# Two reorderings in a split-precision transformer kernel: curve ahead of weight decoding in four steps, and weight sums in two parts

## The chip, the core and the metric

The kernel runs on one core of a Trainium2 chip. The core has a matrix engine (TensorE, PE in the profile, with its weight loads shown apart as PEld), VectorE (DVE), ScalarE (ACT), GpSimd (POOL) and a queue for transfers (SP). Each engine works through its own list of instructions in the order in which the program gives them; an instruction that waits holds up all that stand behind it on that engine. The metric is the device time of one execution in microseconds (us), and less is better.

## The reference, cut to what matters

Three parts follow each other. Shapes are fixed: 2 batches, 8 heads, 768 positions, head width 64, so 1536 tokens of width 512.

```python
def reference(q, k, v, moe_w_in, moe_w_out, moe2_w1, moe2_w2, moe2_w3, moe2_w_out):
    x = local_attention_with_block_summaries(q, k, v)     # [1536, 512]
    h = x @ moe_w_in                                      # [1536, 2048]
    x = (h - tanh(h)) @ moe_w_out                         # [1536, 512]
    a, b = x @ moe2_w1, x @ moe2_w2                       # [1536, 1024] each
    return ((a * b) @ moe2_w3) @ moe2_w_out               # [1536, 512]
```

All of it is in 32-bit floating point.

## The kernel before, in words

**Split products.** TensorE multiplies in a shorter format, so each factor is held as a high part (the value cast down, names ending in `h`) and a low part (what the cast lost, names ending in `l`). A product is three matrix multiplications of 128 x 128 by 128 x 512, high x high, high x low, low x high (`split_mm`, L185 to L188). ScalarE makes a high part, and GpSimd or VectorE subtracts it to make the low part (`low_part`, L190). Where a factor comes from TensorE, both parts must be there before its three multiplications can run: the high part for the first, the low part for the second or the third.

**Weights.** The weights arrive as 64-bit words and are decoded on the chip. The class `Weights` (object `wt`) holds one list of units in the order in which they are needed. One unit is a transfer into a `raw` buffer (a ring of four: a new transfer waits until the decoding of the unit four earlier is over), a first step on ScalarE (L108, in `start`), three on VectorE (L111, L113, L115, in `dve` and `unit`), a cast on ScalarE (L143, in `high`) and a subtraction on GpSimd (L150, in `low`). Nothing schedules this: a unit stands on each engine where the program calls these methods.

**First stage (attention, to about 128 us).** Groups of tiles go through scores, softmax and values, with weight units decoded between them: `wt.start` begins one in each turn of the loop and `wt.dve(1)` three times a turn puts one VectorE step of it between the softmax steps.

**Middle stage (about 128 us to 445 us).** 48 steps, one for each pair of a block of 128 hidden columns `f` and a third of the tokens `k`. Step `n` calls `hidden(n)`: 12 multiplications on TensorE into one of three banks, named `ph`. `curve(n, ...)` then computes h - tanh(h): ScalarE squares (`u`, L530) and takes tanh (`th`, L531), and makes `sq` (L538) and a mask `mk` (L539); VectorE forms a polynomial `g` for small values (L540 to L542) and overwrites it where the mask says so (COPY_PREDICATED, L525). That last operation is put off to the beginning of `curve(n + 1)`, and after it come the high part `gh` of g on ScalarE (L535) and the low part `gl` on GpSimd (L191). `back(n - 2)`, 12 multiplications named `x`, uses them; so TensorE's order is hidden(0), hidden(1), hidden(2), back(0), hidden(3), back(1), hidden(4), and so on. In the first four steps every `hidden` needs a new w_in unit and, from step 2 to step 5, every `back` a new w_out unit; the next new units are needed in step 12.

In the order of the code a step does: `hidden`, `wt.start`, `wt.high`, the reading of finished x banks (`evacuate`), `curve`, `wt.low`, `back`. Inside `curve`, a whole unit is decoded on VectorE (`wt.unit()`, L526) between the predicated copy and the rest.

**Last stage (from about 458 us).** For two of the three thirds of the tokens, a and b are computed with a seven-product scheme in place of eight. `group` (L715) makes one of them, for two blocks of columns: it calls seven products in the order 1, 6, 5, 7, 2, 4, 3, each 6 multiplications into one of four banks named `p_w`, in rotation. VectorE adds a bank to what is to become a block of the result, right behind each product. Product 3 takes the bank that product 5 had; it is read twice, the second time by `tt(c22, c21, add, p5)` (tiles `ab` in the trace), which comes behind product 7. `w_sums` (L689) makes the sums of weights that the next group multiplies with: two operations `t_w` of 512 columns on VectorE, then four of 256 columns (`s_w`), then a cast on ScalarE and a subtraction on GpSimd for each of two results. Products 6 and 5 use the first result, 7 and 3 the second. Group w1 and group w2 alternate for m = 0, 2, 4, 6; both need sums, and each group's sums are made while the group ahead of it runs, directly behind its `yield` after product 5: seven times in all (those of the very first group are made earlier). `between` puts 12 other multiplications (`o`) behind product 5 where there is something to do: in the first group, and from m = 2 in both.

## Time and profile before

| | us |
|---|---|
| median of three runs | 592.7 (590.75 to 592.89) |
| the profiled execution, its own time | 592.24 |
| its span, first to last instruction | 590.4 |
| TensorE busy in the span | 571.6 |
| VectorE busy | 465.4 |
| ScalarE busy | 338.6 |
| GpSimd busy | 278.9 |

The span is the stretch that the trace shows; the execution's own time is 1.84 us longer. A busy share is a mean over stages of different kinds. TensorE's multiplications overlap, and the end that is shown of each is modelled: a multiplication of 512 columns is shown as 0.39 us long, while in a row of them one begins every 0.23 us. In the timeline the bracket behind a row is the engine's idle time ahead of it and what ended that.

### The profile page before, as it was taken

To read this page: it belongs to the slowest core of one execution; us is meant where nothing else is said; L and a number is where in the kernel's file an instruction comes from. 1 tells how busy PE (TensorE), PEld (TensorE's weight loads), DVE (VectorE), ACT (ScalarE), POOL (GpSimd) and SP (SyncE) were. 2 spreads that over 40 slices of the span, in tenths; PEclk is the share of its full clock that TensorE was granted. 3 is DMA by queue.
4 is the path that set the end of the run, shared out by engine and by line. 5 is a ranking of instruction groups with operands and counts; after the bars stand their busy time and mean duration, and the time that the engine had idled before them with its cause. 6 is when DMAs were issued, how large, how long until landed. Compare 5 with 4: busy or idle time off the path is not lost.

```text
span 590.4 us, 9062 instructions
## 1 busy us (share of the span) xinstructions
PE 571.6 (97%) x3168; PEld 461.4 (78%) x3168; DVE 465.4 (79%) x885; ACT 338.6 (57%) x741; POOL 278.9 (47%) x233
## 2 busy tenths in 40 slices
PE   8989999998999999999999999999999999999997
PEld 6667777776888888888888888888887777888885
DVE  3789988789999995779999978999577576878510
ACT  3689977868788774466767667765233322222110
POOL 3456555555556652224645522557735624526120
PEclk9989999998999999999999999999999999999999
DMA  8899996653333230012223102223000100000021
GB/s 323 297 323 306 333 298 226 188 162 111 104 108 108 73 106 1 0 37 73 95 84 101 43 1 64 80 71 108 1 0 1 72 0 1 1 2 0 1 90 53
DMA packets 19678, 59.70 MB, mean 101 GB/s; under 512 B 2096, under 2 KB 4784, under 8 KB 19632
## 3 DMA queue, kind: packets, MB, share of 16 engines
q1 hardware_dynamic: 19632, 59.12, 30.8%
q8 instruction: 25, 0.41, 0.3%
q14 instruction: 21, 0.17, 0.1%
HBM read 54.79 MB, written 3.15 MB: 98 GB/s over the span
## 4 chain that ended last, share of the span: by engine, by line
PE 76%; DVE 14%; issue 6%; POOL 2%; ACT 1%; DMA 1%; DVEq 0%; POOLq 0%; ACTq 0%
PE x L187 6%; PE x L188 6%; PE x L186 6%; PE ph L187 6%; PE ph L188 6%; PE ph L186 6%; PE p_w L186 3%; PE p_w L187 3%; PE p_w L188 3%; PE o L188 3%; PE o L186 3%; PE o L187 3%; PE s L339 2%; PE busy L403 2%; PE w L188 2%
## 5 line engine op out<-in xcount | busy, mean ns | idle before, releaser
L150 POOL TENSOR_TENSOR wl<-dec,wh 128x512 fp32r<-128x512 f32 x72 | 111.5, 1553 | 48.9 <-ACT wh L143 41.6
L191 POOL TENSOR_TENSOR gl<-g,gh 128x512 fp32r<-128x512 f32 x48 | 65.8, 1371 | 140.5 <-ACT gh L535 75.3
L186 PE MATMUL x<-gh,wh 128*128 128x512 f32 x192 | 75.4, 393 | 1.8 <-ACT gh L535 1.8
L187 PE MATMUL x<-gl,wh 128*128 128x512 f32 x192 | 75.5, 393 | 1.0 <-POOL gl L191 1.0
L188 PE MATMUL x<-gh,wl 128*128 128x512 f32 x192 | 75.4, 393 | 0.0
L186 PE MATMUL ph<-xh,wh 128*128 128x512 f32 x192 | 74.8, 390 | 0.0
L187 PE MATMUL ph<-xl,wh 128*128 128x512 f32 x192 | 74.7, 389 | 0.0
L188 PE MATMUL ph<-xh,wl 128*128 128x512 f32 x192 | 74.7, 389 | 0.0
L115 DVE SCALAR_TENSOR_TENSOR dec<-raw,dec 128x512 uint32<-128x512 uint32 x45 | 62.4, 1387 | 1.5
L530 ACT ACTIVATE u<-ph 128x512 f32<-128x512 f32 x48 | 28.8, 600 | 54.8 <-PE ph L188 54.8
L143 ACT CAST wh<-dec 128x512 fp32r<-128x512 f32 x72 | 44.5, 623 | 13.3 <-DVE dec L115 13.2
L540 DVE TENSOR_TENSOR g<-ph,u 128x512 f32<-128x512 f32 x48 | 32.7, 682 | 19.8 <-ACT th L531 19.8
L525 DVE COPY_PREDICATED g<-mk,th 128x512 f32<-128x512 uint32 x48 | 41.7, 870 | 4.0
L186 PEld LDWEIGHTS x<-gh,wh 128*128 128x128 f32 x192 | 36.5, 190 | 10.3 <-ACT gh L535 2.2
L353 ACT ACTIVATE pr<-pr,nm 128x120 f32<-128x120 f32 x96 | 37.0, 390 | 12.1 <-DVE nm L350 11.8
L187 PEld LDWEIGHTS x<-gl,wh 128*128 128x128 f32 x192 | 36.4, 189 | 9.0 <-POOL gl L191 1.3
L188 PEld LDWEIGHTS x<-gh,wl 128*128 128x128 f32 x192 | 36.4, 190 | 7.5
L187 PEld LDWEIGHTS ph<-xl,wh 128*128 128x128 f32 x192 | 36.1, 188 | 7.5
L186 PEld LDWEIGHTS ph<-xh,wh 128*128 128x128 f32 x192 | 36.0, 188 | 7.5
L188 PEld LDWEIGHTS ph<-xh,wl 128*128 128x128 f32 x192 | 36.1, 188 | 7.4
L542 DVE SCALAR_TENSOR_TENSOR g<-sq,g 128x512 f32<-128x512 f32 x48 | 40.3, 839 | 0.7 <-ACT sq L538 0.6
L191 POOL TENSOR_TENSOR s_w<-s_w,s_w 128x512 fp32r<-128x512 f32 x16 | 20.4, 1292 | 38.9 <-ACT s_w L704 36.0
(153 smaller groups left out, 1423.0 us busy)
## 6 DMA issues: line engine op xcount, KB each, us to landing
raw<-w SPq DMA_DIRECT2D x32, 512.0 KB
raw<-w_in SPq DMA_DIRECT2D x16, 512.0 KB
raw<-w_out SPq DMA_DIRECT2D x16, 512.0 KB
vg<-vW SPq DMA_DIRECT2D x8, 768.0 KB
raw<-wo SPq DMA_DIRECT2D x8, 512.0 KB
kt<-kT SPq DMA_DIRECT2D x7, 544.0 KB
vn<-vN SPq DMA_DIRECT2D x8, 384.0 KB
qt<-qT SPq DMA_DIRECT2D x7, 384.0 KB
```

Of the source, the lines that this page charges most:

```text
L115: lambda tu=tu, su=su, lo=lo: stt(out=tu, in0=lo, scalar=29, in1=su, op0=ALU.logical_shift_right, op1=ALU.bitwise_or)])
L143: nc.scalar.copy(out=h, in_=self.t[n])
L150: nc.gpsimd.tensor_tensor(out=l, in0=self.t[self.n_low], in1=h[:, :].bitcast(F32), op=ALU.subtract)
L186: mm(out=acc, lhsT=lh, rhs=rh, start=start, stop=False)
L187: mm(out=acc, lhsT=lh, rhs=rl, start=False, stop=False)
L188: mm(out=acc, lhsT=ll, rhs=rh, start=False, stop=stop)
L191: eng.tensor_tensor(out=out, in0=x, in1=high.bitcast(F32), op=ALU.subtract)
L353: nc.scalar.activation(out=pr[g][:, i, :], in_=pr[g][:, i, :], func=AF.Exp, scale=-1.0, bias=nm[g][:, i:i + 1], accum_out=z[g][:, i:i + 1])
L525: nc.vector.copy_predicated(out=g, mask=mask[:, :].bitcast(U32), data=t)
L530: nc.scalar.activation(out=u, in_=ph, func=AF.Square)
L540: nc.vector.tensor_tensor(out=gn, in0=ph, in1=u, op=ALU.mult)
L542: nc.vector.scalar_tensor_tensor(out=gn, in0=sq, scalar=GAM, in1=gn, op0=ALU.add, op1=ALU.mult)
```

## The change

The change touches three places.

In the attention's last turn no weight unit is begun and no VectorE step of one is put between the softmax steps.

In the first four steps of the middle stage (`FIRST = 4`), `curve` stands ahead of `wt.start`; the high and low parts of the step before follow directly behind the predicated copy, ahead of the new `u` and `th`; and no unit is decoded inside `curve`. Steps 2 and 3 decode one unit each behind `curve`, and steps 0 and 1 none; `wt.high` is called from step 2 on. From step 4 on all is as it was.

In the last stage `w_sums` is a generator in two parts. The two `t_w` operations stand where they were; the four `s_w`, with the casts and subtractions behind them, follow only after product 7 has been added and the bank of product 5 has been read.

```diff
+FIRST = 4
...
-                    if i:
+                    if i and g < NG + 3:
                         wt.dve(1)
...
-                wt.start(2 if g in MORE else 1)
+                if g < NG + 3:
+                    wt.start(2 if g in MORE else 1)
...
         def curve(n, ph, prev):
 
+            def high():
+                gp[n - 1] = tmp("gh", n, LAG + 1, F32R), tmp("gl", n, LAG + 1, F32R)
+                nc.scalar.copy(out=gp[n - 1][0], in_=g)
+                low_part(nc.gpsimd, gp[n - 1][1], g, gp[n - 1][0][:, :])
+
             if prev is not None:
                 mask, t, g = prev
                 nc.vector.copy_predicated(out=g, mask=mask[:, :].bitcast(U32), data=t)
-            wt.unit()
+                if n < FIRST:
+                    high()
+            if n >= FIRST:
+                wt.unit()
...
-            if prev is not None:
-                gp[n - 1] = tmp("gh", n, LAG + 1, F32R), tmp("gl", n, LAG + 1, F32R)
-                nc.scalar.copy(out=gp[n - 1][0], in_=g)
-                low_part(nc.gpsimd, gp[n - 1][1], g, gp[n - 1][0][:, :])
+            if prev is not None and n >= FIRST:
+                high()
...
+            if n < FIRST:
+                cur = curve(n, nxt, cur)
             wt.start()
...
-            wt.high()
+            if LAG <= n < FIRST:
+                wt.unit()
+            if n >= LAG:
+                wt.high()
             closing = len(evac)
             evacuate()
-            cur = curve(n, nxt, cur)
+            if n >= FIRST:
+                cur = curve(n, nxt, cur)
             wt.low()
...
             for t, h, l in ((t0, h0, l0), (t1, h1, l1)):
                 tt(t, h[:, :].bitcast(F32), add, l[:, :].bitcast(F32))
+            yield
             a, b = slice(0, H * P), slice(H * P, DM)
...
-            return lhs
+            yield lhs
...
             next(g)
-            lhs = w_sums("w2", m)
-            for _ in range(4):
+            sums = w_sums("w2", m)
+            next(sums)
+            next(g)
+            lhs = next(sums)
+            for _ in range(3):
                 next(g, None)
...
-            if m + 2 < NM:
-                lhs = w_sums("w1", m + 2)
+            more = m + 2 < NM
+            if more:
+                sums = w_sums("w1", m + 2)
+                next(sums)
             for a, b in ((a22, b22), (a11, b11), (a21, b21)):
                 next(g)
+                if more and a is a22:
+                    lhs = next(sums)
                 tt(a, a, ALU.mult, b)
```

The order on TensorE and on SP is the same before and after. On ScalarE, at the beginning of the middle stage, this stands before (numbers behind names only tell buffers apart; `dec_1943` and `dec_1958` are the w_out units of back(2) and back(3), `wh_1948` that of back(1)):

```order
L143 CAST wh_1948<-dec_1903 128x512
L108 ACTIVATE dec_1958<-raw_1896 128x512
L108 ACTIVATE dec_1997<-raw_1901 128x512
L143 CAST wh_1999<-dec_1943 128x512
L530 ACTIVATE u_2007<-ph_1984 128x512
L531 ACTIVATE th_2009<-ph_1984 128x512
L538 ACTIVATE sq_2008<-u_2007,nsb 128x512
L539 ACTIVATE mk_2010<-u_2007,numax 128x512
L108 ACTIVATE dec_2033<-raw_1941 128x512
L143 CAST wh_2035<-dec_1958 128x512
L530 ACTIVATE u_2044<-ph_2020 128x512
L531 ACTIVATE th_2046<-ph_2020 128x512
```

And this stands there after (`wh_2071` further down is now the cast of `dec_1943`):

```order
L144 CAST wh_1948<-dec_1903 128x512
L540 ACTIVATE u_1990<-ph_1977 128x512
L541 ACTIVATE th_1992<-ph_1977 128x512
L546 ACTIVATE sq_1991<-u_1990,nsb 128x512
L547 ACTIVATE mk_1993<-u_1990,numax 128x512
L109 ACTIVATE dec_2002<-raw_1896 128x512
L527 CAST gh_2018<-g_1994 128x512
L540 ACTIVATE u_2022<-ph_2004 128x512
L541 ACTIVATE th_2024<-ph_2004 128x512
```

The first `u` has moved ahead of two first steps of units and of a cast that waits for VectorE, and the first `gh` ahead of the second `u`.

On VectorE, at the same place before, behind the decoding of back(1)'s unit:

```order
L111 TENSOR_SCALAR dec_1943<-dec_1943 128x512
L191 TENSOR_TENSOR xl_122<-av_1920,xh_119 128x256
L113 SCALAR_TENSOR_TENSOR dec_1943<-raw_1853,dec_1943 128x512
L115 SCALAR_TENSOR_TENSOR dec_1943<-raw_1853,dec_1943 128x512
L111 TENSOR_SCALAR dec_1958<-dec_1958 128x512
L113 SCALAR_TENSOR_TENSOR dec_1958<-raw_1896,dec_1958 128x512
L115 SCALAR_TENSOR_TENSOR dec_1958<-raw_1896,dec_1958 128x512
L540 TENSOR_TENSOR g_2011<-ph_1984,u_2007 128x512
L541 TENSOR_TENSOR th_2009<-ph_1984,th_2009 128x512
L542 SCALAR_TENSOR_TENSOR g_2011<-sq_2008,g_2011 128x512
L525 COPY_PREDICATED g_2011<-mk_2010,th_2009 128x512
```

After, from the polynomial of step 1 to the predicated copy at the head of step 3 (that of step 0 stands ahead in the same way, with nothing of a unit in front of it):

```order
L548 TENSOR_TENSOR g_2026<-ph_2004,u_2022 128x512
L549 TENSOR_TENSOR th_2024<-ph_2004,th_2024 128x512
L550 SCALAR_TENSOR_TENSOR g_2026<-sq_2023,g_2026 128x512
L532 COPY_PREDICATED g_2026<-mk_2025,th_2024 128x512
L548 TENSOR_TENSOR g_2058<-ph_2036,u_2054 128x512
L549 TENSOR_TENSOR th_2056<-ph_2036,th_2056 128x512
L550 SCALAR_TENSOR_TENSOR g_2058<-sq_2055,g_2058 128x512
L112 TENSOR_SCALAR dec_1943<-dec_1943 128x512
L114 SCALAR_TENSOR_TENSOR dec_1943<-raw_1853,dec_1943 128x512
L116 SCALAR_TENSOR_TENSOR dec_1943<-raw_1853,dec_1943 128x512
L532 COPY_PREDICATED g_2058<-mk_2057,th_2056 128x512
```

The two units that stood ahead of the first polynomial now stand behind the third and the fourth; all later units follow three steps later than they did.

On VectorE in the last stage, group w2 of m = 0, this stands before (`p_w_0_5085` is the bank of product 5, `p_w_0_5110` that of product 7):

```order
L668 TENSOR_TENSOR b_5067<-b_5067,p_w_0_5085 128x512
L668 TENSOR_TENSOR t_w_2_5093<-wh_4214,wl_4215 128x512
L668 TENSOR_TENSOR t_w_2_5094<-wh_4332,wl_4333 128x512
L668 TENSOR_TENSOR s_w_2_5095<-t_w_2_5094 128x256
L668 TENSOR_TENSOR s_w_2_5095<-s_w_2_5095,t_w_2_5093 128x256
L668 TENSOR_TENSOR s_w_2_5096<-t_w_2_5093,t_w_2_5094 128x256
L668 TENSOR_TENSOR s_w_2_5096<-t_w_2_5093,s_w_2_5095 128x256
L668 TENSOR_TENSOR b_5067<-b_5067,p_w_0_5110 128x512
L668 TENSOR_TENSOR ab_1_4969<-b_5067,p_w_0_5085 128x512
L668 TENSOR_TENSOR ab_0_4968<-ab_0_4968,ab_1_4969 128x512
```

And after (product 7's bank is now `p_w_0_5099`):

```order
L682 TENSOR_TENSOR b_5067<-b_5067,p_w_0_5085 128x512
L682 TENSOR_TENSOR t_w_2_5093<-wh_4214,wl_4215 128x512
L682 TENSOR_TENSOR t_w_2_5094<-wh_4332,wl_4333 128x512
L682 TENSOR_TENSOR b_5067<-b_5067,p_w_0_5099 128x512
L682 TENSOR_TENSOR ab_1_4969<-b_5067,p_w_0_5085 128x512
L682 TENSOR_TENSOR s_w_2_5095<-t_w_2_5094 128x256
L682 TENSOR_TENSOR s_w_2_5095<-s_w_2_5095,t_w_2_5093 128x256
L682 TENSOR_TENSOR s_w_2_5096<-t_w_2_5093,t_w_2_5094 128x256
L682 TENSOR_TENSOR s_w_2_5096<-t_w_2_5093,s_w_2_5095 128x256
L682 TENSOR_TENSOR ab_0_4968<-ab_0_4968,ab_1_4969 128x512
```

The four `s_w` have moved behind the second reading of product 5's bank; the product of a and b (`ab_0_4968`), and the additions behind it, keep their places behind the sums. In the groups w1 the same two rows change places with the four, and in the first of them two copies of finished outputs move ahead with them.

## Rows read from the trace of the kernel before

**Rows 1.** The page's busy times of the engines, us, share of span, instructions.

```profile
PE 571.6 (97%) x3168; PEld 461.4 (78%) x3168; DVE 465.4 (79%) x885; ACT 338.6 (57%) x741; POOL 278.9 (47%) x233
```

**Rows 2.** Waits of TensorE: line, whom for, us in total, times, longest.

```profile
PE p_w L186 <- DVE ab L668: 3.2, 3, 1.4
PE x L186 <- ACT gh L535: 1.8, 1, 1.8
```

**Rows 3.** Stretches: length, busy us of each engine, granted clock, DMA share.

```profile
137.00:144.72 7.72, 4.94 (x15) 3.50 (x13) 7.38 (x12) 5.86 (x11) 3.47 (x3) 0.78 0.36 132
140.50:144.00 3.50, 3.50 (x9) 2.72 (x10) 3.36 (x7) 2.16 (x5) 1.65 (x1) 0.52 0.40 138
...
150.00:200.00 50.00, 50.00 (x222) 41.43 (x221) 48.42 (x65) 41.08 (x73) 29.51 (x20) 1.00 0.32 95
```

**Rows 4.** Timeline of TensorE, first steps of the middle stage: start, length, instruction.

```profile
131.40 0.39 PE L188 MATMUL ph<-xh,wl 128*128 128x512 f32 x1
...
136.84 0.39 PE L188 MATMUL ph<-xh,wl 128*128 128x512 f32 x1
...
144.72 0.39 PE L186 MATMUL ph<-xh,wh 128*128 128x512 f32 x1
```

**Rows 5.** Timeline of ScalarE, first steps of the middle stage.

```profile
133.45 0.59 ACT L530 ACTIVATE u<-ph 128x512 f32<-128x512 f32 x1
...
135.03 0.72 ACT L539 ACTIVATE mk<-u,numax 128x512 f32<-128x512 f32 x1
...
138.32 0.62 ACT L535 CAST gh<-g 128x512 fp32r<-128x512 f32 x1 [0.52 <-DVE g L525]
```

**Rows 6.** Timeline of VectorE, first steps, and the decoding of a later unit.

```profile
133.99 1.67 DVE L115 SCALAR_TENSOR_TENSOR dec<-raw,dec 128x512 uint32<-128x512 uint32 x1
...
136.78 0.68 DVE L542 SCALAR_TENSOR_TENSOR g<-sq,g 128x512 f32<-128x512 f32 x1
137.56 0.73 DVE L525 COPY_PREDICATED g<-mk,th 128x512 f32<-128x512 uint32 x1
...
165.13 0.41 DVE L111 TENSOR_SCALAR dec<-dec 128x512 uint32<-128x512 uint32 x1
...
166.30 0.69 DVE L115 SCALAR_TENSOR_TENSOR dec<-raw,dec 128x512 uint32<-128x512 uint32 x1
```

**Rows 7.** Timeline of GpSimd, first steps of the middle stage.

```profile
139.02 1.43 POOL L191 TENSOR_TENSOR gl<-g,gh 128x512 fp32r<-128x512 f32 x1 [3.91 <-DMA raw<-w_out]
```

**Rows 8.** Timeline of TensorE in the last stage, where product 3 begins.

```profile
469.35 0.39 PE L188 MATMUL p_w<-xh,wl 128*128 128x512 f32 x1
470.63 0.50 PE L186 MATMUL p_w<-xh,s_w 128*128 128x512 f32 x1 [0.90 <-DVE ab L668]
...
481.41 0.50 PE L186 MATMUL p_w<-xh,s_w 128*128 128x512 f32 x1 [0.87 <-DVE ab L668]
...
495.42 0.50 PE L186 MATMUL p_w<-xh,s_w 128*128 128x512 f32 x1 [1.38 <-DVE ab L668]
```

**Rows 9.** Timeline of VectorE in the last stage, two groups.

```profile
475.16 0.69 DVE L668 TENSOR_TENSOR b<-u_b,p_w 128x512 f32<-128x512 f32 x1 [2.15 <-PE p_w L188]
...
478.48 0.42 DVE L668 TENSOR_TENSOR s_w<-t_w 128x256 f32<-128x256 f32 x1
...
479.95 0.68 DVE L668 TENSOR_TENSOR b<-b,p_w 128x512 f32<-128x512 f32 x1
480.67 0.69 DVE L668 TENSOR_TENSOR ab<-b,p_w 128x512 f32<-128x512 f32 x1
481.39 1.83 DVE L668 TENSOR_TENSOR ab<-ab,ab 128x512 f32<-128x512 f32 x1
...
494.68 0.69 DVE L668 TENSOR_TENSOR ab<-a,p_w 128x512 f32<-128x512 f32 x1
```

**Rows 10.** Timeline of ScalarE, then GpSimd, in the last stage.

```profile
479.40 1.29 ACT L704 CAST s_w<-s_w 128x512 fp32r<-128x512 f32 x2 [5.13 <-DVE s_w L668]
...
480.15 2.52 POOL L191 TENSOR_TENSOR s_w<-s_w,s_w 128x512 fp32r<-128x512 f32 x2 [9.57 <-ACT s_w L704]
```

More of the change, by code (lines that the diff above doesn't have):

```diff
@@ L749, in fused_kernel @@
                 wt.free += [(rawp, "raw", "raw", NRAW)] * NRAW
-                lhs = w_sums("w1", 0)
+                _, lhs = w_sums("w1", 0)
             a = product_a(m, 0)
```

## The prediction

> **What bounds the kernel now.** I read the busy times first. TensorE is busy for 571.6 of 590.4 us [rows 1], so only its idle or slow time can be gained; the other engines matter where it waits for them. The waits of TensorE come second: of those that the change touches, three at product 3 (3.2 us, for the second reading of product 5's bank) and one at the first `back` (1.8 us, for `gh`) stand out [rows 2]. The stretches are third, since a wait can also cost clock: from 137.00 to 144.72 us TensorE is busy for 4.94 of 7.72 us at a mean granted clock of 0.78, and from 140.50 to 144.00 the clock is 0.52, its lower level (1.2 GHz); before and from 144 us on the trace shows 1.00 [rows 3]. Last come the timelines of the four engines around these two places [rows 4 to 10].
>
> **First steps of the middle stage.** From one last multiplication of a `hidden` to the next but one are 24 multiplications, 131.40 to 136.84, so one begins every 0.227 us, and 12 take 2.72 [rows 4]. hidden(2) leaves its last place at 136.84 + 0.23 = 137.07, and hidden(3) begins at 144.72. back(0) needs 2.72 of these 7.65 us; 4.93 are lost: 2.78 idle (7.72 less 4.94 [rows 3]) and some 2.1 at the lower clock.
>
> What TensorE waits for begins with `u` at 133.45 [rows 5], although hidden(0)'s last multiplication ended at 131.40 + 0.39 = 131.79 [rows 4]: `u` stood behind a cast that waited for a unit on VectorE, and VectorE's polynomial stood behind one more, whose last step took 1.67 us from 133.99 [rows 6]. Both units are needed only by back(2) and back(3). The change takes both out of the way. I follow the new chain with the durations of before.
>
> Step 0: `u` begins at 131.83. `mk` begins 1.58 later (135.03 less 133.45) and ends 0.72 after that, at 134.13 [rows 5]. VectorE's third operation needs `sq`, which I put at 0.62 ahead of `mk`'s end; so it starts at about 133.66, and the predicated copy 0.78 later (137.56 less 136.78), ending after 0.73, at 135.17 [rows 6]. `gh` follows 0.03 later and takes 0.62: 135.82. `gl` starts 0.70 behind the start of `gh` and takes 1.43 [rows 5, 7]: 137.33. back(0)'s first multiplication, due at 137.07, has its `gh`; the second, due at 137.30, has its `gl` at 137.37. About 0.1 us is lost in place of 4.93.
>
> Steps 1 to 3: from `u` to the next `u` is 3.9 (the 3.37 to `gh`, and ScalarE's next place 0.53 on), less than the 5.44 that TensorE gives to a step. So `u` starts at 135.7 and 139.6, and gl(1) ends at 141.2, for a place at 142.5. The third polynomial ends at 142.1; now the unit of back(2) comes on VectorE: from the first step to the end of the last 1.86 (166.30 + 0.69 less 165.13), or 2.84 where the last step takes 1.67 [rows 6]. I take 1.86, because GpSimd has nothing between gl(1) and this unit. Then come copy and `gh`, to 145.4, and on GpSimd the unit's low part first, 144.7 to 146.0, and gl(2) to 147.4, for a place at 148.2: 0.8 to spare, or 0.2 late. Step 3 in the same way: `u` 145.3, polynomial 147.8, unit 149.7, copy 150.4; but now ScalarE has the cast, a unit's first step, `u` and `th` of step 4 ahead of gh(3) (step 4 has the old order), to 152.4; and gl(3) to 153.9, for a place at 153.7. Here 0.2 is lost, 1.2 if both units took the longer time. Together 0.3 lost, bounds 0.1 and 3.8 (0.1 + 0.2 + 1.2 + a slow clock as before, 2.1, with 0.2 for its restart): this part gains **4.6**, between 1.1 and 4.8.
>
> Behind step 3 VectorE's work per step is as before, and nearly all its time (48.42 of 50.00 us [rows 3]); since it starts with TensorE, both are earlier by the same amount. The units come three steps later than they did. The order on GpSimd shows that each low part stands at least two steps, 10.9 us, ahead of its use. The transfers wait for a raw buffer and shift with the units: that for step 4 is released at 144.0, and ScalarE asks for it at about 150. Cost zero, hidden by these distances. Leaving out the unit at the attention's end moves three VectorE operations out of a stretch where TensorE isn't waiting: zero, with 0.2 either way.
>
> **Last stage.** In a row a multiplication is shown 0.39 long but takes 0.23, so each wait costs the idle time, 0.16, and 0.11 for the slower start (its 0.34 to the next in place of 0.23, from rows like that of 470.63). The three cost 0.90, 0.87 and 1.38 plus 0.27 each [rows 8]: 1.17, 1.14 and 1.65, together 3.96. What is moved is four operations, 478.48 to 479.95, 1.47 us [rows 9].
>
> In group w1 of m = 0 the second reading ends 1.47 earlier, at 469.1, and product 3 is due at 469.35 + 0.23 = 469.58 [rows 8]: nothing is left of the wait. In w2 of m = 0 it ends at 480.67 + 0.69 - 1.47 = 479.9, for a place at 480.4: nothing left. So TensorE reaches w1 of m = 2 earlier by 2.31. There the reading ended at 494.68 + 0.69 = 495.37 [rows 9]. VectorE runs nearly without a gap from w2 of m = 0 to this point, and its chain begins with a wait of 2.15 for TensorE [rows 9]; so it comes 1.17 earlier, and 1.47 by the move, while TensorE comes 2.31 earlier to a place that was 1.54 before the reading. The place is at 491.6 and the reading at 492.7. Part of the 1.83 of the product (0.69 in other rows of its kind) may go too, since the product then starts 0.2 ahead of GpSimd's subtractions: GpSimd began 1.67 behind the first `s_w` (480.15 less 478.48 [rows 9, 10]), the product would come 1.47 behind it. I credit half a us: 492.2, so 0.6 remains, with 0.27 for its ends; the third wait goes from 1.65 to 0.9.
>
> What is late next are the sums themselves. They feed product 6 of the next group, and the additions behind them free its banks. From the end of the reading the first sum's low part takes 0.9 on VectorE, 0.65 on ScalarE (1.29 for two [rows 10]) and 1.26 on GpSimd (2.52 for two), with their handovers 3.0; TensorE gets to the place in product 6 that uses it 13 to 14 multiplications later, 3.3 after a product 3 that waited and more otherwise. It fits, closely. In the later groups w2, where VectorE used to make the sums while it waited for product 7, they now delay what follows by 1.5, and the next reading comes earlier by 1.47: I charge 0.1 each for w1 of m = 4 and m = 6. Sum: 1.17 + 1.14 + 0.75 - 0.2 = **2.8**, bounds -1.3 (below) and 4.0.
>
> 4.6 + 2.8 = 7.4 off the profiled execution's own 592.24 (span 590.4) gives 584.8. Its time is 0.46 below the runs' median, and I put the forecast at **585.0**.
>
> A rule speaks against the second part. The Trainium skill, "GPSIMD Engine Reference", section "1. Specifications", says that GpSimd's way into SBUF is shared with VectorE, which collides with it when it has two inputs there. The trace agrees: the product of two SBUF tiles took 1.83 us beside GpSimd's subtractions, and the additions that read a bank 0.68 and 0.69 [rows 9, 10]. Whether it costs here hangs on which of the two begins first, and that is a rival of its own.
>
> **The rivals.**
> A. The wait at the first steps only moves. The late units collide with GpSimd, gl(2) and gl(3) miss their places, and the clock falls again: the lower bound, 1.1, in place of 4.6. For it: gl(3) has no room by my own chain. Against: GpSimd is idle when either unit is decoded. 592.24 - 1.1 - 2.8 = 588.3.
> B. GpSimd's subtractions begin ahead of the product, which then waits for both (2.52) in w2 of m = 0, 2 and 4; the addition behind it frees product 2's bank for the next product 6 some 2 us late. I take 1.3 to 1.5 off each time, 4.1 in all: 2.8 - 4.1 = -1.3, and 592.24 - 4.6 + 1.3 = 588.9. For it: the 1.83. Against: 0.2 us in the product's favour.
> C. A and B: 592.24 - 1.1 + 1.3 = 592.4.
> D. Slower: product 6 waits for the moved sums in all seven groups that have them, each time by the whole 1.47 and 0.11: 11.1, against 7.4 gained: 595.9. It takes over 1.5 us in each to be slower than can be told from no change. For it: 0.3 to spare in one group. Against: 0.8 and more in the others by the same count.
>
> **How the numbers follow.** My forecast 0.64 (583.2 to 587.2), A 0.15, B 0.12, C 0.06, D 0.03. The range 583.2 to 589.8 takes in nearly all of the first three. What can be told from no change is about 0.5%, 3.0 us: below 589.7 is faster. That is the forecast, most of A and B: 0.86; C and the rest 0.11; D 0.03.
>
> **What would show it.** hidden(3) should begin at about 139.8 instead of 144.72, back(0) without a gap, and no stretch at the lower clock there; hidden(6) at 156.5 or so (A: at 159 or later, with waits for `gl`). The first `u` should follow hidden(0) directly. In the last stage two of the three waits for `ab` should be gone and the third be about half as long; the product in w2 of m = 0 should last about 0.7 (B: 1.5 or more, and product 6 waiting for the reading of product 2's bank). Waits of product 6 for a low part would speak for D. I'm wrong if hidden(3) still begins after 142, or product 3 still waits at m = 0.

## The result and the profile after

The changed kernel took 585.41 us (median of four runs, 584.81 to 586.69), the kernel before 592.73 beside it: a ratio of 0.9876, 95% interval 0.9853 to 0.9899. In a second comparison (median of six runs) it was 586.83 against 592.12: 0.9910, interval 0.9888 to 0.9932. The forecast was 585.0, from 583.2 to 589.8, and the time lies near it. The two terms of its sum were further off: the first was too large by more than two us, the second too small by almost one.

To see this, the runs have to be cut into stages, since the first stage (attention) begins the second at another moment in each execution: hidden(0) began between 127.2 and 130.9 us in the fourteen profiles of this study, whether the attention's last turn was the old or the new one. From hidden(0) on, the stages repeat to some hundredths of a us. "Middle" is the time from the first multiplication of hidden(0) to the first one named `p_w`, "last" from there to the end of the span:

| kernel | hidden(0) | middle | last | middle + last |
|---|---|---|---|---|
| before | 128.77 | 329.74 | 131.89 | 461.63 |
| after | 129.07 | 327.52 | 128.31 | 455.83 |
| after, second profile | 128.70 | 327.50 | 128.30 | 455.80 |

So the change gained 2.22 us in the middle and 3.58 in the last stage, 5.8 in all (0.990 of the time before), where 4.6 and 2.8 were forecast. The medians differ by 7.3 in one comparison and by 5.3 in the other. The two stages repeat and cannot make these 2 us; the attention stage can, which the change leaves as good as alone.

One thing that moves the attention stage is TensorE's clock. In every one of the fourteen profiles TensorE waits there, to about 31 us, 1.49 or 1.50 us for `kt` of GpSimd. In eight of them the granted clock is at its lower level (1.2 GHz) for 3.4 us soon behind this wait, and hidden(0) began at 128.77 or later; in the other six it is not, and hidden(0) began at 128.70 or earlier. The two profiles of the kernel after are one of each kind. TensorE's wait and the window behind it (columns as in [rows 3], the clock is the number ahead of the last two), in the first profile and then in the second:

```profile
31.10 0.73 PE L340 MATMUL s<-kt,qt 64*64 64x120 f32 x10 [1.50 <-POOL kt L309]
31.75:35.17 3.42, 3.42 (x15) 2.42 (x12) 2.04 (x8) 2.40 (x10) 2.23 (x2) 0.50 0.89 225
```

```profile
31.63 0.83 PE L340 MATMUL s<-kt,qt 64*64 64x120 f32 x12 [1.49 <-POOL kt L309]
31.90:35.32 3.42, 3.42 (x44) 2.70 (x42) 2.90 (x13) 3.32 (x12) 2.25 (x2) 1.00 0.86 234
```

The mean granted clock of the whole execution was 0.997 in the first of these and 1.000 in the second. It was 0.999 or 1.000 in three of the four executions behind the median of 585.41, and in one of the six behind 586.83. So the first median probably owes part of its lead to the attention stage; this is argued from the mean clocks, since the other executions have no trace. Waits for transfers differ in that stage too, so the clock is not all of it.

TensorE's busy time is nearly that of before [rows 1], and the waits for `gh` and `ab` [rows 2] are gone from the list. The page's busy line and the wait of TensorE that takes their place (line, whom for, total, times, longest):

```profile
PE 570.1 (97%) x3168; PEld 460.1 (79%) x3168; DVE 460.8 (79%) x885; ACT 338.7 (58%) x741; POOL 280.3 (48%) x233
```

```profile
PE x L188 <- POOL gl L192: 1.7, 2, 1.3
```

Before, TensorE waited for `gl` once, 1.0 us in back(0); now it does so twice, and one of the two is long. The same stretch as in [rows 3], and the long one that holds the new wait, with the columns as there:

```profile
137.00:144.72 7.72, 7.41 (x33) 5.83 (x32) 5.17 (x9) 5.23 (x10) 2.31 (x2) 1.00 0.00 0
150.00:200.00 50.00, 48.64 (x214) 39.70 (x213) 48.49 (x67) 40.42 (x72) 28.06 (x18) 1.00 0.29 98
```

In the first stretch TensorE is busy for 7.41 of 7.72 us at the full clock, where it was busy for 4.94 at 0.78. But from 150 to 200 us, where it had no gap, it now lacks 1.36. TensorE's timeline shows both places: the first multiplication of hidden(0), the wait in back(0), the start of hidden(3), the wait in back(3), the start of hidden(6), and that of the last stage.

```profile
129.07 0.50 PE L187 MATMUL ph<-xh,wh 128*128 128x512 f32 x1
...
137.37 0.39 PE L187 MATMUL x<-gh,wh 128*128 128x512 f32 x1
138.07 0.50 PE L188 MATMUL x<-gl,wh 128*128 128x512 f32 x1 [0.31 <-POOL gl L192]
...
140.69 0.39 PE L187 MATMUL ph<-xh,wh 128*128 128x512 f32 x1
...
154.69 0.49 PE L187 MATMUL x<-gh,wh 128*128 128x512 f32 x1
156.53 0.50 PE L188 MATMUL x<-gl,wh 128*128 128x512 f32 x1 [1.35 <-POOL gl L192]
...
159.18 0.39 PE L187 MATMUL ph<-xh,wh 128*128 128x512 f32 x1
...
456.59 0.39 PE L187 MATMUL p_w<-xh,wh 128*128 128x512 f32 x1
```

hidden(3) begins 11.62 us behind hidden(0), where it was 15.95: 4.33 are gained there. hidden(6) begins 30.11 behind it, and before 32.27 (128.77 to 161.04): 2.16 are left, and 2.22 at the stage's end. Half of what was gained at the first wait was lost again by the third step behind it, most of it at gl(3).

ScalarE, then VectorE, then GpSimd, in the first and in the fourth and fifth step:

```profile
132.13 0.60 ACT L540 ACTIVATE u<-ph 128x512 f32<-128x512 f32 x1 [1.25 <-PE ph L189]
132.62 0.59 ACT L541 ACTIVATE th<-ph 128x512 f32<-128x512 f32 x1
...
136.03 0.62 ACT L527 CAST gh<-g 128x512 fp32r<-128x512 f32 x1 [1.02 <-DVE g L532]
136.55 0.59 ACT L540 ACTIVATE u<-ph 128x512 f32<-128x512 f32 x1
...
151.97 0.62 ACT L144 CAST wh<-dec 128x512 fp32r<-128x512 f32 x1 [2.04 <-DVE dec L116]
152.49 0.67 ACT L109 ACTIVATE dec<-raw 128x512 f32<-128x512 f32 x1
153.07 0.57 ACT L540 ACTIVATE u<-ph 128x512 f32<-128x512 f32 x1
...
154.03 0.61 ACT L527 CAST gh<-g 128x512 fp32r<-128x512 f32 x1
```

```profile
133.25 0.69 DVE L548 TENSOR_TENSOR g<-ph,u 128x512 f32<-128x512 f32 x1 [2.70 <-ACT th L541]
...
154.65 0.69 DVE L116 SCALAR_TENSOR_TENSOR dec<-raw,dec 128x512 uint32<-128x512 uint32 x1
```

```profile
152.66 1.40 POOL L151 TENSOR_TENSOR wl<-dec,wh 128x512 fp32r<-128x512 f32 x1 [3.55 <-ACT wh L144]
154.77 1.71 POOL L192 TENSOR_TENSOR gl<-g,gh 128x512 fp32r<-128x512 f32 x1 [0.70 <-PE ph L189]
```

In the last stage VectorE reads product 5's bank a second time (`ab`) ahead of the four `s_w`, and the product of two tiles that took 1.83 [rows 9] takes 0.69, because it now starts 0.2 ahead of GpSimd's two subtractions, which took 2.52 [rows 10] and take 3.34:

```profile
475.96 0.69 DVE L682 TENSOR_TENSOR ab<-b,p_w 128x512 f32<-128x512 f32 x1
476.57 0.42 DVE L682 TENSOR_TENSOR s_w<-t_w 128x256 f32<-128x256 f32 x1
...
478.03 0.69 DVE L682 TENSOR_TENSOR ab<-ab,ab 128x512 f32<-128x512 f32 x1
...
489.29 0.69 DVE L682 TENSOR_TENSOR ab<-a,p_w 128x512 f32<-128x512 f32 x1
```

```profile
478.23 3.34 POOL L192 TENSOR_TENSOR s_w<-s_w,s_w 128x512 fp32r<-128x512 f32 x2 [7.06 <-issue]
```

The reading that the third wait was for (group w1 of m = 2) stood 36.17 us behind the stage's start (494.68 less 458.51) and stands 32.70 behind it now (489.29 less 456.59). Product 3 of that group still begins a little late, too little for the list of waits: it was due 0.23 behind 489.59, at 489.82.

```profile
489.59 0.39 PE L189 MATMUL p_w<-xh,wl 128*128 128x512 f32 x1
490.03 0.50 PE L187 MATMUL p_w<-xh,s_w 128*128 128x512 f32 x1
```

### The profile page after: what moved, and what is told of

Its sections match the earlier page's. It is cut to its first block, busy times and chain, and to the rows that moved or that the text cites. A ratio compares the mean times of both kernels' runs of the same rounds, so it can differ in the third digit from the quotient of the medians.

```text
span 584.9 us, 9056 instructions
## 1 busy us (share of the span) xinstructions
PE 570.1 (97%) x3168; PEld 460.1 (79%) x3168; DVE 460.8 (79%) x885; ACT 338.7 (58%) x741; POOL 280.3 (48%) x233
## 4 chain that ended last, share of the span: by engine, by line
PE 80%; DVE 10%; ACT 3%; DMA 2%; issue 2%; POOL 1%; SPq 0%; DVEq 0%; POOLq 0%; ACTq 0%
PE x L188 7%; PE x L187 7%; PE x L189 7%; PE ph L187 7%; PE ph L189 7%; PE ph L188 7%; PE p_w L187 4%; PE p_w L189 4%; PE p_w L188 4%; PE o L189 3%; PE o L187 3%; PE o L188 3%; PE busy L404 2%; PE w L189 2%; PE w L188 2%
## 5 line engine op out<-in xcount | busy, mean ns | idle before, releaser
L116 DVE SCALAR_TENSOR_TENSOR dec<-raw,dec 128x512 uint32<-128x512 uint32 x45 | 59.6, 1325 | 1.5
L192 POOL TENSOR_TENSOR s_w<-s_w,s_w 128x512 fp32r<-128x512 f32 x16 | 22.9, 1450 | 43.5 <-ACT s_w L719 23.5
```

The costliest lines, as they stand in the source:

```text
L116: lambda tu=tu, su=su, lo=lo: stt(out=tu, in0=lo, scalar=29, in1=su, op0=ALU.logical_shift_right, op1=ALU.bitwise_or)])
L192: eng.tensor_tensor(out=out, in0=x, in1=high.bitcast(F32), op=ALU.subtract)
```

## The experiments

Expected and measured, in the order in which they ran. The times without an interval are single runs; the stages are read from each kernel's profile as above.

| kernel | hidden(0) | middle | last | time | ratio to before, interval |
|---|---|---|---|---|---|
| e1_middle | 129.26 | 327.50 | 131.84 | 590.55 | 0.9979 (0.9957 to 1.0002) |
| e2_sums | 127.21 | 329.72 | 128.27 | 588.31 | 0.9937 (0.9916 to 0.9958) |
| e3_first5 | 127.87 | 326.99 | 128.34 | 585.68 | 0.9891 (0.9868 to 0.9913) |
| e4_tail | 129.25 | 328.61 | 128.34 | 587.27 | 0.9917 (0.9898 to 0.9937) |
| after_again | 128.70 | 327.50 | 128.30 | 586.83 | 0.9910 (0.9888 to 0.9932) |
| e10_tail3 | 129.39 | 326.76 | 128.25 | 585.86 | 0.9899 (0.9872 to 0.9925) |
| e6_sq | 128.17 | 332.18 | 128.25 | 590.44 | |
| e7_later | 129.21 | 327.50 | 131.19 | 589.65 | |
| e11_both | 128.88 | 327.26 | 128.36 | 586.10 | 0.9893 (0.9873 to 0.9913) |
| e12_gh3 | 127.78 | 328.00 | 128.32 | 585.86 | |
| e8_w1only | 128.34 | 327.52 | 128.84 | 586.50 | |
| e9_w2only | 130.90 | 327.48 | 134.52 | 594.64 | |

**Each half alone.** e1_middle has the last stage of the kernel before:

```
-            sums = w_sums("w2", m)
-            next(sums)
-            next(g)
-            lhs = next(sums)
+            lhs = w_sums("w2", m)
...
```

> Only the first part of the change (the attention's last turn and the first four steps of the middle stage); the last stage is that of the kernel before. Theory 1, the prediction's two terms as they stand: 4.6 us gained here, 592.7 - 4.6 = 588.1. Theory 2, the terms as the one profile after shows them (hidden(6) 1.9 us earlier, with a wait of 1.35 for gl(3)): 592.7 - 1.9 to 2.2, 590.5 to 590.8, and the three waits at product 3 of the last stage stand as before, 3.2 us in all. The third matmul of hidden(6) should show which: about 157.4 by theory 1, 159.2 to 159.6 by theory 2.

e2_sums has the attention and the middle stage of before, and keeps those lines.

> Only the last part of the change (the sums of weights in two parts); the attention and the middle stage are those of the kernel before. Theory 1, the prediction's term: 2.8 us gained, 592.7 - 2.8 = 589.9, with a third wait at product 3 (w1, m = 2) of about 0.6 us. Theory 2, the profile after: all three waits gone, 3.6 to 3.9 gained, 588.8 to 589.1. The wait of 1.8 us for gh(0) and the lower clock between 140.5 and 144 us stay in both.

Theory 2 holds in both: 2.24 us in the middle (329.74 less 327.50), 3.62 in the last stage (131.89 less 128.27), but for the small rest of the third wait, which is there in e2_sums too (0.22). The two halves do not touch each other, and their sum is the whole. In the runs the last part is told from no change and the first isn't quite: its interval just reaches 1. Waits of TensorE in e1_middle, then in e2_sums:

```profile
PE p_w L187 <- DVE ab L682: 3.1, 3, 1.4
```

```profile
PE x L186 <- ACT gh L535: 1.8, 1, 1.8
...
PE x L187 <- POOL gl L191: 1.0, 1, 1.0
```

**The wait for gl(3).** e3_first5 keeps the new order for a step more:

```
-FIRST = 4
+FIRST = 5
+LAST_UNIT = 4
...
-            if LAG <= n < FIRST:
+            if LAG <= n < LAST_UNIT:
                 wt.unit()
```

> The kernel after with the new order kept for one more step (step 4: curve first, gh and gl ahead of the new u and th), and no unit decoded in that step; units are decoded in steps 2 and 3 as after. Theory 1: gl(3) is late (1.35 us) because gh(3) stands behind a unit's first step, u and th of step 4 on ScalarE; then gh(3) starts at about 152.6 instead of 154.03, the wait for gl(3) falls to 0.2 or less and the time by about 1.2: 585.4 - 1.2 = 584.2. Theory 2: VectorE is simply behind in these steps, and the wait moves on to gl(4), where the old order begins: 585.4, with a wait of 1 us or more in back(4).

The wait fell to 0.36, near theory 1. But the edit does two things: gh(3) no longer stands behind u and th on ScalarE, and VectorE no longer decodes a unit beside gl(3), which took 1.29 in place of 1.71. e12_gh3, below, does the first alone, and there the wait fell only to 0.89. hidden(6) began 28.83 behind hidden(0) (after: 30.11). Of the 1.28 only 0.53 are left at the end of the stage: the unit that step 4 leaves out is decoded later, and at 236.80 TensorE waits for VectorE's reading of an x bank, where the kernel after lost nothing between 165 and 300 us (135.00 us busy of 135):

```profile
154.06 0.50 PE L189 MATMUL x<-gl,wh 128*128 128x512 f32 x1 [0.36 <-POOL gl L193]
```

```profile
236.80 0.50 PE L188 MATMUL x<-gh,wh 128*128 128x512 f32 x1 [0.38 <-DVE x2a L577]
```

**The attention's last turn.** e4_tail puts it back as it was:

```
-                    if i and g < NG + 3:
+                    if i:
                         wt.dve(1)
...
-                if g < NG + 3:
-                    wt.start(2 if g in MORE else 1)
+                wt.start(2 if g in MORE else 1)
```

> The kernel after with the attention's last turn as it was before (a unit is begun there, and VectorE decodes one there that after decodes only in step 2). Theory 1, the prediction's zero for that edit: 585.4 within 0.2, gl(3) late as after, since a unit is still decoded in each of steps 2 and 3. Theory 2: the VectorE operations put back stand ahead of the polynomial of step 0 and put gh(0), and so hidden(3), back by 1 to 1.7 us: 586.4 to 587.1.

Neither: hidden(3) begins as after (11.66 behind hidden(0)), but gl(2) is now 0.96 late beside gl(3)'s 1.33, and the middle takes 1.1 more. The unit that the attention decodes has its low part on GpSimd in step 2, just where VectorE decodes the next one; the first decoding step took 1.52 in place of 0.42, until GpSimd was done. VectorE, then GpSimd:

```profile
144.13 1.52 DVE L112 TENSOR_SCALAR dec<-dec 128x512 uint32<-128x512 uint32 x1
```

```profile
144.04 1.33 POOL L151 TENSOR_TENSOR wl<-dec,wh 128x512 fp32r<-128x512 f32 x1 [1.41 <-ACT wh L144]
```

So the edit that the prediction put at zero is worth 1.1 here, half of the gain in the middle.

**The kernel after again.** No edit.

> The kernel after once more, to stand beside the next one on the same chip. If the profile after is typical, the stretch from hidden(0) to the first product of the last stage lasts 327.5 us again (329.7 before), and the stretch from there to the end 128.3 (131.9 before): a gain of 5.8 us, some 0.990 of the time of before. If the 7.3 us between the first medians were typical, the ratio would be 0.9876.

Both stages repeat to 0.02 us, and the ratio is nearer to theirs, 0.990, than to that of the first comparison.

**One unit less.** e10_tail3 is e4_tail without a unit in step 2:

```
-            if LAG <= n < FIRST:
+            if LAG < n < FIRST:
                 wt.unit()
```

> The kernel after with the attention's last turn as before (it decodes a unit) and no unit decoded in step 2 (only in step 3), so that VectorE has one unit less among the first four polynomials. Theory 1: gl(3) is late because each unit among the first steps holds the chain of copy, gh, next u back by its 1.86 us; with one less, u(3) starts 1.5 to 1.9 us earlier, the waits for gl(2) and gl(3) go, and the stretch from hidden(0) to the last stage lasts 326.0 to 326.3 instead of 327.5. Theory 2: gl(3) is late because of what stands ahead of gh(3) on ScalarE in step 4 alone (a unit's first step, u and th); then a wait of 0.8 or more for gl(3) stays, 327.0 or more.

Neither bound was met, 326.76 lies between, and theory 2 has the wait: gl(2) was in time, but gl(3) fell only from 1.32 to 1.08. u(3) came 0.73 earlier after hidden(0) than after (17.27 against 18.00), not 1.5 to 1.9, because the predicated copy ran into GpSimd's low part (1.65 in place of 0.76, at 144.45).

**What the polynomial waits for.** e6_sq swaps two operations of ScalarE:

```
                 nc.scalar.activation(out=u, in_=ph, func=AF.Square)
+                if n < FIRST:
+                    nc.scalar.activation(out=sq, in_=u, ...)
                 nc.scalar.activation(out=t, in_=ph, func=AF.Tanh)
```

> The kernel after with ScalarE's order u, sq, th, mk in place of u, th, sq, mk in the first four steps; VectorE's order is unchanged. After, VectorE's first polynomial operation started 1.12 us behind the start of u, at the end of th. Theory 1, it waits for th by its semaphore: it starts 1.7 behind u now, gh(0) comes 0.5 to 0.6 later, and hidden(3) begins 0.3 to 0.6 later after hidden(0) than after (11.62). Theory 2, it can't read the bank ph while th reads it, but needs u alone: 0.65 behind u, beside sq. Theory 3, what ScalarE has written needs 0.5 more to be seen by VectorE: 1.12 as after.

Theory 1: VectorE's first operation starts at 133.09, 1.87 behind u and 0.03 behind the end of th. ScalarE, then VectorE:

```profile
131.22 0.60 ACT L540 ACTIVATE u<-ph 128x512 f32<-128x512 f32 x1 [1.25 <-PE ph L189]
131.85 0.72 ACT L542 ACTIVATE sq<-u,nsb 128x512 f32<-128x512 f32 x1
132.48 0.58 ACT L543 ACTIVATE th<-ph 128x512 f32<-128x512 f32 x1
```

```profile
133.09 0.69 DVE L551 TENSOR_TENSOR g<-ph,u 128x512 f32<-128x512 f32 x1 [3.44 <-ACT th L543]
```

From u to u it is 5.18 instead of 4.42, and hidden(3) begins 12.36 behind hidden(0), a little more than theory 1 had. With the units of steps 2 and 3 on top, TensorE waits 1.42 in back(2) and 0.79 and 1.32 in back(3), and the clock falls for 3.4 us behind that: the middle takes 4.7 us more than after, 2.4 more than before.

**Rival B, made to happen.** e7_later puts the product one operation later:

```
                     lhs = next(sums)
-                tt(a, a, ALU.mult, b)
+                    continue
+                if a is a11:
+                    tt(a22, a22, ALU.mult, b22)
+                tt(a, a, ALU.mult, b)
```

> The kernel after with the product ab = a times b of each group w2 put one operation later on VectorE, behind the addition after product 2, so that it starts behind GpSimd's subtractions and not ahead of them. Theory 1, the prediction's rival B: the product then waits for GpSimd (about 1.8 to 2.5 instead of 0.69 in m = 0), the addition behind it frees product 2's bank late, and the last stage takes 1.3 us or more per group w2, up to 4.1, longer than the 128.3 us of after. Theory 2: VectorE has slack here, the price stays on VectorE, and the last stage lasts 128.3 to 128.6.

Theory 1: 131.19, 2.9 us more for three groups. The product took 1.44 and the next one 1.77, and product 6 of the next group waited for the reading of its bank, 0.87, 0.27 and 0.37. VectorE, then TensorE:

```profile
478.76 1.44 DVE L682 TENSOR_TENSOR ab<-ab,ab 128x512 f32<-128x512 f32 x1
480.12 1.77 DVE L682 TENSOR_TENSOR sq_a<-sq_a,u_b 128x512 f32<-128x512 f32 x1
```

```profile
482.55 0.50 PE L187 MATMUL p_w<-xh,s_w 128*128 128x512 f32 x1 [0.87 <-DVE b L682]
```

**A better version?** e11_both is e10_tail3 with gh(3) ahead of u and th in step 4; e12_gh3 is the kernel after with that edit:

```
-                if n < FIRST:
+                if n <= FIRST:
                     high()
...
-            if prev is not None and n >= FIRST:
+            if prev is not None and n > FIRST:
                 high()
```

> The kernel with the attention's last turn as before and no unit in step 2 (the one that took 326.8 us from hidden(0) to the last stage), and in step 4 gh(3) and gl(3) ahead of the new u and th; the unit of step 4 stays ahead of the polynomial. Theory 1, gh(3) stood behind u and th on ScalarE: gh(3) starts 1.0 earlier, gl(3) is bound by the low part ahead of it on GpSimd, its wait falls from 1.08 to about 0.2, and the stretch lasts 325.8 to 326.0 us, 1.5 to 1.7 less than the kernel after; the time then is 0.987 to 0.988 of that of before. Theory 2, u and th of step 4, now 0.5 later, hold back gl(4) and the wait moves one step on: 326.6 or more.

> The kernel after with that last edit alone: in step 4 gh(3) and gl(3) ahead of the new u and th. Theory 1: the wait for gl(3) falls from 1.32 to 0.5 (gl(3) follows the low part of the unit on GpSimd at once), and the stretch from hidden(0) to the last stage lasts 326.6 to 326.8 us instead of 327.5. Theory 2: the wait moves to gl(4), 327.4 or more.

The first half of theory 1 came true in e11_both: the wait for gl(3) fell to 0.41, and hidden(6) began 28.65 behind hidden(0), 1.46 earlier than after. But then back(4) needed banks that ScalarE had not yet copied, and neither theory had that: the copies stand behind a cast that waits for VectorE's unit. In e12_gh3 the wait for gl(3) fell to 0.89 and the same bank cost 0.86; it ends 0.5 behind the kernel after, within theory 2's bound, but by the bank and not by gl(4). TensorE in e11_both, then ScalarE:

```profile
161.96 0.50 PE L187 MATMUL x<-gh,wh 128*128 128x512 f32 x1 [0.86 <-ACT x2a L573]
```

```profile
160.81 0.62 ACT L144 CAST wh<-dec 128x512 fp32r<-128x512 f32 x1 [0.31 <-DVE dec L116]
161.33 2.04 ACT L573 COPY x2a<-x 128x512 f32<-128x512 f32 x4
```

By its stages e10_tail3 is the best (455.0 against 455.8); its runs and those of the kernel after, 585.86 and 586.83 in one comparison, have intervals that overlap, so it isn't shown to be faster.

**The sums of one kind of group alone.** e8_w1only splits only the sums that are made in a group w1, e9_w2only only those made in a group w2:

```
# e8_w1only, in a group w2
                 next(sums)
+                lhs = next(sums)
...
-                if more and a is a22:
-                    lhs = next(sums)
# e9_w2only, in a group w1
             next(sums)
-            next(g)
             lhs = next(sums)
+            next(g)
```

> The kernel after with the sums in two parts only where they are made in a group w1; those made in a group w2 stand as before, ahead of the additions. The last stage took 131.9 us before and 128.3 after. Theory 1: each wait goes by its own move of 1.47, so the first (w1, m = 0) and the third (w1, m = 2, 1.38 long) are gone and the second (w2, m = 0, 0.87) stays: 129.2 to 129.5. Theory 2, the prediction's account: the third went only because the product in w2 became short (0.69 instead of 1.83); then 0.5 or more of it stays here: 129.7 or more.

> The kernel after with the sums in two parts only where they are made in a group w2; those made in a group w1 stand as before. Theory 1, each wait goes by its own move: the first wait (0.90) stays, the second (0.87) is gone, the third stays and grows by what TensorE is now earlier than VectorE (1.4 to 1.8): 130.6 to 131.1 us for the last stage. Theory 2, the short product in w2 brings VectorE forward by as much as the move: the third wait falls to 0.9 or less: 130.3 or less.

Theory 1 holds in e8_w1only: the first and the third wait are gone, the second stays (0.88), and 3.05 of the 3.58 us are there without the short product, which is 1.83 long as before. In e9_w2only the third wait grew to 1.71 as theory 1 says, but two more appeared that no theory had, at m = 4 and m = 6, and the last stage took 2.6 us more than before:

```profile
470.50 0.50 PE L187 MATMUL p_w<-xh,s_w 128*128 128x512 f32 x1 [0.90 <-DVE ab L682]
...
494.70 0.50 PE L187 MATMUL p_w<-xh,s_w 128*128 128x512 f32 x1 [1.71 <-DVE ab L682]
...
521.13 0.50 PE L187 MATMUL p_w<-xh,s_w 128*128 128x512 f32 x1 [1.38 <-DVE ab L682]
...
547.52 0.50 PE L187 MATMUL p_w<-xh,s_w 128*128 128x512 f32 x1 [1.43 <-DVE ab L682]
```

Why these two come is argued, not shown: moving work of a group w2 behind its readings brings those readings forward and puts the additions after them back, into the next group w1, whose own sums still stand ahead of its second reading.

## Why the prediction was right, and where it was not

**Term 1, 4.6 forecast, 2.2 measured: the step "from u to the next u is 3.9".** The prediction let VectorE's polynomial begin as soon as u was there, and took only sq and mk as what could hold it back. It waits for th as well, though its first operation doesn't read it: 1.12 behind u, and e6_sq moved it with th. (The chain as recorded also holds 0.15 that no row gives: its `sq` ends at 133.51 and its third operation starts at 133.66.) Every step is thus 0.5 longer, 4.42 (132.13 to 136.55) instead of 3.9. That isn't visible in [rows 5, 6], where VectorE came later anyway, but the waits of the kernel before had the row, and it wasn't read:

```profile
DVE g L540 <- ACT th L531: 19.8, 13, 2.3
```

At step 0 this costs little: gl(0) was ready 0.7 later than forecast (138.01 for 137.33, of which 0.3 is the later start of the stage), and back(0) lasted 3.32 in place of 2.72. By step 4 it has added up. gh(3) was put at 151.8 and started at 154.03; less the 0.3 that is 1.9 late: 1.0 from the two steps without a unit, 0.9 from the two with one, 6.1 and 6.0 from u to u, which is more than the 5.44 that TensorE gives to a step. Then gl(3) took 1.71 beside VectorE's decoding, more than the 1.43 of [rows 7]. The wait that was put at 0.2 with a bound of 1.2 was 1.35. The remaining loss is small: 0.2 each in back(2) and hidden(5). Together 2.8 lost (0.60 + 0.22 + 0.18 + 1.77 of back(3)) in place of 0.3.

**Rival A was half right.** The wait moved, as A had it, to gl(3), where the old order begins, and its sign (hidden(6) at 159 or later, with waits for `gl`) was met by a hair: 159.18, of which 0.3 is the later start of the stage. But A's reason was another: the two late units met nothing on GpSimd and took 1.87 us each on VectorE (143.96 to 145.83, 150.06 to 151.93), as the forecast had them. And the clock, 2.3 us of A's price, stayed at 1.00. What was lost without either was 2.8 us where A had 1.5. e3_first5, e10_tail3 and e11_both show that each mend of that wait keeps 0.2 to 0.8 us and, in two of the three, uncovers another; e12_gh3, the fourth, lost 0.5 by the one it uncovered.

**Term 2, 2.8 forecast, 3.6 measured: the rest of the third wait.** What the three waits cost was forecast as 3.96, and the trace of before bears it out: the gaps of 1.28, 1.26 and 1.77, less 0.23 each, and 0.11 for each slower start behind them. The first two went as worked out. The third was to go from 1.65 to 0.9 and went to 0.32: 0.21 for product 3 and 0.11 for the slower start. The reading came 3.47 us earlier in the stage (36.17 less 32.70), where 1.17 + 1.47 + 0.5 = 3.14 had been put. The half us credited for the short product was not too small: the product took 1.14 less, but the next two products of tiles on VectorE took 1.07 each where they had taken 0.69, so that 0.4 was left. The 0.2 charged for m = 4 and m = 6 wasn't taken; 0.2 was lost elsewhere, at 483.3, where TensorE needs a low part (`gl_c`) that GpSimd ends at 483.29. e8_w1only shows that the move of its own group is enough for the third wait, of which it has nothing left. The move in w2 adds only 0.5 to that (128.84 less 128.32): its own wait, 1.14, less the 0.32 and the 0.2 that come with it.

**Rivals B and D.** The 0.2 us by which the product was to come ahead of GpSimd came out as forecast (478.03 and 478.23), and e7_later shows the price of losing them: 2.9, where 4.1 had been taken from the lengths of the operations. D's waits for a moved sum appeared nowhere. The Trainium skill, "SBUF — State Buffer", section "SBUF: two separate sides", says that the port pair which VectorE and GpSimd share is an exclusive lock, held for a whole instruction by whichever starts first, where VectorE's instruction is in a 2-port perf mode or has two inputs in SBUF. The traces agree for two inputs: the product that began first took 0.69 and GpSimd's two subtractions behind it 3.34 in place of 2.52, and the one of e7_later that began second took 1.44. The decoding step of e4_tail has one input and was held too: it began 0.09 behind GpSimd's subtraction, took 1.52 and ended 0.28 behind it; which mode it ran in, no run shows.

**The edit at zero.** Leaving out the unit at the attention's end was put at zero because TensorE wasn't waiting there. It isn't zero: what counts is where that unit's low part runs, two steps later. e4_tail puts it at 1.1.

**The total.** 2.4 too much and 0.8 too little made 7.4 into 5.8, and 592.24 less 5.8 is 586.4. That the first median came within 0.4 us of the forecast is luck twice over: the two errors have opposite signs, and these four runs stood 7.3 below those of before, 1.5 more than the stages give, where the next six stood 5.3 below.

## What to carry to other kernels

Before you chain a step's durations, list for each operation in the chain everything that it waited for anywhere in the program: one line of the waits of before held the half us per step that was missing here. When the first wait of a start-up goes, look where the work that was taken out of its way is put back, and whether the steps there are longer than the bound engine's step; half of the gain can come back as a wait a few steps on. Two edits of the same kind in alternating groups are not a sum: one alone was worth most of it, the other alone made the last stage longer than before.

## What was not expected of the hardware

A wait of much the same length cost the clock in one place and not in the next. Behind the wait of 1.35 us for gl(3) TensorE stayed at its full clock (2.4 GHz): the granted clock was 1.00. Behind the 1.49 or 1.50 us for `kt` in the attention it fell to its lower level (1.2 GHz) in eight profiles and not in six, and the two profiles of the kernel after, the same program, differ in this. Before, 1.77 and 1.02 us of idle with one multiplication between them were followed by 3.5 us at 0.52, and in e6_sq waits of 0.79 and 1.32 us close together by 3.7 us at 0.64. In e4_tail waits of 0.96 and 1.33 us some 6 us apart were not: the clock was 1.00 from 148 to 159 us. Windows of the kernel after, then of e6_sq, columns as in [rows 3]:

```profile
156.53:159.18 2.65, 2.65 (x12) 2.17 (x13) 2.48 (x6) 1.97 (x4) 0.39 (x1) 1.00 0.48 186
```

```profile
156.00:158.80 2.80, 0.69 (x3) 0.37 (x3) 2.77 (x5) 2.80 (x6) 1.84 (x2) 1.00 0.50 151
158.80:162.46 3.66, 3.66 (x11) 2.87 (x12) 3.49 (x5) 3.02 (x6) 1.60 (x2) 0.64 0.36 134
```

So the two places where the middle stage had two waits close together paid for them twice, in idle time and in clock, and the waits that stood alone in it did not pay in clock. That this will hold elsewhere is not shown, and the wait for `kt` shows that one execution does not settle what a wait costs.
